# Three instead of eight transfers in flight at the start of the SyncE queue, in a fused retention and two-layer MoE kernel

## The chip, the cores and the metric

The kernel runs on one core of a Trainium2 chip. The metric is device time in microseconds (us); lower is better. Engines are named as in the profile: PE is TensorE, PEld its weight loads, DVE VectorE, ACT ScalarE, POOL GpSimd, SP SyncE. SP does no arithmetic here: it issues nearly all DMA transfers, in program order.

## The reference

```python
# attention with decay, B=4, H=8, S=768, D=64
for t in range(S):
    state = gamma * state + outer(k[:, :, t], v[:, :, t])
    y[:, :, t] = scale * (q[:, :, t] @ state)
x = y as 3072 tokens x 512
# first layer, d_ff 1024
h = x @ w_in
solu = h * softmax(h)
x = layernorm(solu) * g_ln @ w_out
# second layer, d_ff 2048
h = x @ w_in2
out = (h * cos(h)) @ w_out2
```

## The kernel before

The sequence is cut into chunks of 64 tokens. A step handles one chunk of two batches: scores of the chunk (`sc`, L394), the running state (`S`, L400), and the output from both (`y` or, for step 1, `hA`, L412), each as many 64x64 matmuls. There are 24 steps. Their results, split into a rounded and a remainder part (`xh`, `xl`), feed the first layer (L605, into `hA` and `hB`), whose weights `w1h` and `w1l` are made on the chip: raw words come into `big` (L478), ACT and DVE shift them together, ACT writes the rounded half (`w1h`) and DVE the remainder (`w1l`, L341). Later parts (L674, L851, L934, L936) are the rest of the two layers.

The order of all instructions is not written by hand. `Plan.add` records operations with their duration and their dependencies, and `Plan.order` (L117) plays them against a small model of the engines and of the DMA queue and emits them in that order. For DMA it holds that a transfer can start when the eighth before it has landed (`LANES`, L59, used at L169). The chip is held to the same rule by the semaphores: eight of them tell of landings, and each transfer waits for the earlier one that used its semaphore. Two of the first ones belong to constants that ACT issues (L366, L368).

Each step loads two transfers of 512 KB, the first with keys and queries ("kq"), the second with keys and values ("kv") (`load_step`, L357 to L368); there are four input buffers. A weight transfer (L478) is 511.8 KB. The start of the program is

```python
load_to(0)
load_to(2)
weights(2)
load_to(3)
weights(6)
```

so the first transfers of SP are, counted from 0: step 0 (0, 1), step 1 (2, 3), step 2 (4, 5), two weights (6, 7), step 3 (8, 9), six weights (10 to 15), steps 4 to 7 (16 to 22 and one more), with a small constant `gcol` (L504) close to the end.

Of the kernel before, what the change touches and what calls it, by code (L numbers as in the profile page):

```python
# [46 lines left out]
class Plan:  # L47
# [16 lines left out]
    STEP = 0.05  # L64
    LOOK = .1
    FIRST = (16, 0.96, 0.6)

    def __init__(self):
        self.ops = []
        self.alts = {}  # L70
        self.bulk = set()
        self.chain = False
        self.last = []
        self.keys = []
        self.writers = {}
        self.readers = {}
# [40 lines left out]
    def order(self):  # L117
        ops = self.ops
        n = len(ops)
        succ = [[] for _ in ops]  # L120
        need = [0] * n
        for i, o in enumerate(ops):
            need[i] = len(o[3])
            for d, full in o[3]:
                succ[d].append((i, full))
        last = None
        nxt = [None] * n
        for i, o in enumerate(ops):
            if o[0] == "PE":
                if last is not None:  # L130
                    nxt[last] = i
                last = i
        rank = [0.0] * n
        for i in range(n - 1, -1, -1):
            eng, occ, _, _, lat, _, xfer = ops[i]
            if i in self.alts and self.alts[i][1] < occ:
                lat -= occ - self.alts[i][1]
                occ = self.alts[i][1]
            tail = lat + self.SEM + (self.LEAD + xfer + self.LAND if xfer else 0)
            best = occ  # L140
            for s, full in succ[i]:
                best = max(best, rank[s] + (tail if full else 0))
            if nxt[i] is not None:
                best = max(best, rank[nxt[i]] + occ)
            rank[i] = best
        ready_at = [0.0] * n
        start = [None] * n
        free = {e: 0.7 for e in ("PE", "ACT", "DVE", "POOL", "SP", "HOOK")}
        pools = {e: [] for e in free}
        pe = [i for i, o in enumerate(ops) if o[0] == "PE"]  # L150
        port = [0.0, None]
        dma = 2.65
        begun = 0
        lanes = [0.0] * self.LANES

        def ready(i):
            if need[i] == 0 and ops[i][0] != "PE":
                pools[ops[i][0]].append(i)
                if i in self.alts:
                    pools[self.alts[i][0]].append(i)  # L160

        def begin(i, e):

            occ, prt = (ops[i][1], ops[i][5]) if e == ops[i][0] else (self.alts[i][1], self.alts[i][3])
            t = max(free[e], ready_at[i])
            if prt and port[1] != e:
                t = max(t, port[0])
            if ops[i][6]:
                t = max(t, lanes[-self.LANES])  # L169
                if i in self.bulk:  # L170
                    t = max(t, dma - self.BEHIND)
            return t, occ

        for i in range(n):
            ready(i)
        left = n
        out = []
        while left:
            best = None
            for e in free:  # L180
                if e == "PE":
                    c = []
                    for k, i in enumerate(pe[:self.WINDOW]):
                        if need[i] == 0:
                            t = max(free[e], ready_at[i])
                            c.append((max(free[e], ready_at[i] + self.MARGIN) + k * self.STEP, t, i))
                    if not c:
                        continue
                    _, t, i = min(c)
                    if best is None or t < best[0]:  # L190
                        best = (t, e, i)
                    continue
                else:
                    c = []
                    for i in pools[e]:
                        t, occ = begin(i, e)
                        if i in self.alts:
                            t2, occ2 = begin(i, self.alts[i][0] if e == ops[i][0] else ops[i][0])
                            if t2 + occ2 < t + occ - 1e-9:
                                continue  # L200
                        c.append((t, i))
                    if not c:
                        continue
                t0 = min(t for t, _ in c)
                pick = min((i for t, i in c if t <= t0 + self.LOOK), key=lambda i: -rank[i])
                t0 = next(t for t, i in c if i == pick)
                if best is None or t0 < best[0]:
                    best = (t0, e, pick)
            t, e, i = best
            eng, occ, _, _, lat, prt, xfer = ops[i]  # L210
            if e != eng:
                _, occ, _, prt = self.alts[i]
                lat = occ + 0.09
            if e == "PE":
                pe.remove(i)
            else:
                pools[eng].remove(i)
                if i in self.alts:
                    pools[self.alts[i][0]].remove(i)
            start[i] = t  # L220
            free[e] = t + occ
            if prt:
                port = [t + occ, e]
            done = t + lat + self.SEM
            if xfer:
                begun += 1
                boot = begun <= self.FIRST[0]
                if boot:
                    xfer *= self.FIRST[1]
                dma = max(dma, t + occ + self.LEAD) + xfer  # L230
                done = dma + self.LAND + (self.FIRST[2] if boot else self.LATE if i in self.bulk else 0.0)
                lanes.append(done)
            for s, full in succ[i]:
                need[s] -= 1
                ready_at[s] = max(ready_at[s], done if full else t)
                ready(s)
            out.append(self.alts[i][2] if e != eng else ops[i][2])
            left -= 1
        self.start = start
        self.end = max(s + o[4] for s, o in zip(start, ops))  # L240
        return out
# [3 lines left out]
def body(ctx: ExitStack, tc: tile.TileContext, qkv, consts,  # L245
# [3 lines left out]
    P = Plan()  # L249
# [80 lines left out]
        nc.gpsimd.memset(t, 0)  # L330
    make_identity(nc, ident)

    def dma(fn, size, r=(), w=(), occ=0.47, eng="SP", after=(), bulk=False):
        rows, row = size
        return P.add(eng, occ, fn, r, w, xfer=rows / 16 * max(0.046, row / 24.5e3), after=after, bulk=bulk)

    def act(out, in_, func, r, w, occ, lat=None, alt=None, **kw):
        return P.add("ACT", occ, lambda: nc.scalar.activation(out=out, in_=in_, func=func, **kw), r, w, lat, alt=alt)  # L338
# [18 lines left out]
    def load_step(n):  # L357

        bp, i = steps[n]
        for h, x in enumerate(("kq", "kv")):  # L360
            c = slice(2 * h, 2 * h + 2)
            dma(lambda h=h, c=c: nc.sync.dma_start(
                out=a_in[n % NA][:, c], in_=qkv[bp, i, :, h * 1024:h * 1024 + 1024].rearrange("p (c f) -> p c f", f=512)),
                (128, 4096), w=[("in", n % NA, x)])
            if n == 0 and h == 0:
                dma(lambda: nc.scalar.dma_start(out=c_all[:, 0:352], in_=consts[:, 0:352]), (128, 1408), w=[("cs",)], eng="ACT")  # L366
            if n == 1 and h == 0:
                dma(lambda: nc.scalar.dma_start(out=c_all[:, 352:608], in_=consts[:, 352:608]), (128, 1024), w=[("gat",)], eng="ACT")  # L368
# [881 lines left out]
```

## Time and profile before

| what | value |
|---|---|
| three runs | 825.86, 826.69, 828.76 us; median 826.69 |
| the profiled execution's own time | 827.25 us |
| its span, first to last instruction | 825.5 us |
| PE busy | 809.2 us, 98% of the span |
| DVE busy | 685.2 us, 83% |
| ACT busy | 504.6 us, 61% |
| HBM traffic | 226 GB/s over the span |

The span is the time between the first and the last instruction of the profiled execution; what lies around it makes up the rest of its own time. A busy share is an average over stages. A row of waits tells what ended the idle time of an engine; "issue" is time in which the engine waited for nothing that the profile shows.

### The profile page before, as it was taken

The numbers are of one execution on the slowest core, as the hardware profiler recorded it, in microseconds if no ns is written. First come the engines' busy times: TensorE is split into PE (matmuls) and PEld (weight loads), VectorE is DVE, ScalarE is ACT, GpSimd is POOL, SyncE is SP. The second block draws the span as 40 slices with busy tenths as digits, with TensorE's granted clock in tenths as the row PEclk, the third lists the DMA queues.
The fourth block names the chain that finished last, engine by engine and source line by source line (L and its number), as shares of the span: only waits on it lengthen the run. The fifth ranks groups of instructions, "written<-read, shape, count | busy, mean of one in ns | idle before, by whom it ended". The sixth has DMA issues, their size and how long they took to land.

```text
span 825.5 us, 17746 instructions
## 1 busy us (share of the span) xinstructions
PE 809.2 (98%) x6652; PEld 682.4 (83%) x6652; DVE 685.2 (83%) x1269; ACT 504.6 (61%) x908; POOL 48.5 (6%) x55
## 2 busy tenths in 40 slices
PE   4999999999999999999999999999999999999998
PEld 4788888888888888788888888888888888888887
DVE  4799978889888677449999996899999949989975
ACT  3789856656666466346686563666846546665453
POOL 2131201101101000000000000000000000000000
PEclk9999999999999999999999999999999999999999
DMA  9894799999976638247666779766657696666664
GB/s 346 333 333 143 259 306 295 320 288 293 330 264 226 222 161 308 90 133 197 193 205 189 215 209 283 241 193 195 203 187 227 195 283 199 192 194 190 187 190 98
DMA packets 93509, 188.12 MB, mean 228 GB/s; under 512 B 9712, under 2 KB 25328, under 8 KB 93424
## 3 DMA queue, kind: packets, MB, share of 16 engines
q1 hardware_dynamic: 92816, 186.41, 70.8%
q8 instruction: 53, 0.87, 0.4%
q10 hardware_dynamic: 608, 0.57, 0.2%
q14 instruction: 32, 0.26, 0.1%
HBM read 145.01 MB, written 41.94 MB: 226 GB/s over the span
## 4 chain that ended last, share of the span: by engine, by line
PE 95%; DMA 2%; DVE 1%; issue 1%; SPq 0%; ACT 0%; DVEq 0%
PE U L851 28%; PE hA L605 14%; PE y L674 12%; PE pa L934 10%; PE U L934 8%; PE pa L936 5%; PE y L412 4%; PE U L936 4%; PE tr L650 2%; PE hB L605 2%; PE tr L674 2%; PE sc L394 1%; DMA wr<-wd 1%; PE S L400 1%; DMA raw<-y1d 1%
## 5 line engine op out<-in xcount | busy, mean ns | idle before, releaser
L879 ACT ACTIVATE gh<-A 128x512 fp32r<-128x512 f32 x168 | 106.2, 632 | 94.6 <-PE pa L934 48.2
L881 DVE TENSOR_TENSOR gl<-A,gh 128x512 fp32r<-128x512 f32 x168 | 114.6, 686 | 13.5 <-ACT gh L879 11.3
L674 PE MATMUL y<-lt,o1h 128*128 128x512 f32 x304 | 102.1, 399 | 0.0
L934 PE MATMUL pa<-wr,gh 128*128 128x512 f32 x372 | 101.6, 394 | 0.0
L888 DVE TENSOR_TENSOR A<-A,A 128x512 f32<-128x512 f32 x120 | 81.0, 684 | 0.7
L934 PE MATMUL U<-wr,gh 128*128 128x512 f32 x288 | 78.6, 394 | 0.0
L934 PEld LDWEIGHTS pa<-wr,gh 128*128 128x128 f32 x372 | 63.9, 189 | 8.9
L674 PEld LDWEIGHTS y<-lt,o1h 128*128 128x128 f32 x304 | 57.1, 188 | 12.6 <-ACT ys L679 0.3
L605 PE MATMUL hA<-w1h,xh 128*128 128x512 f32 x160 | 64.5, 403 | 0.2 <-DVE u L349 0.2
L936 PEld LDWEIGHTS pa<-wr,gl 128*128 128x128 f32 x372 | 57.2, 189 | 8.0
L605 PE MATMUL hA<-w1h,xl 128*128 128x512 f32 x160 | 62.6, 391 | 0.0
L605 PE MATMUL hA<-w1l,xh 128*128 128x512 f32 x160 | 62.5, 391 | 0.0
L936 PE MATMUL pa<-wr,gl 128*128 128x256 f32 x372 | 59.4, 281 | 0.0
L674 PE MATMUL y<-lt,o1l 128*128 128x512 f32 x152 | 59.3, 390 | 0.0
L338 ACT ACTIVATE st<-wt 128x512 fp32r<-128x512 f32 (+1 forms) x60 | 35.7, 600 | 36.3 <-DMA wd<-st 24.6
L341 DVE TENSOR_TENSOR st<-wt,st 128x512 fp32r<-128x512 f32 (+1 forms) x60 | 41.2, 689 | 18.4 <-ACT st L338 18.1
L934 PEld LDWEIGHTS U<-wr,gh 128*128 128x128 f32 x288 | 49.3, 189 | 6.6
L936 PEld LDWEIGHTS U<-wr,gl 128*128 128x128 f32 x288 | 44.2, 188 | 6.1
L412 PE MATMUL y<-s,in 64*64 64x64 f32 x736 | 45.0, 226 | 1.6 <-DVE s L341 1.6
L936 PE MATMUL U<-wr,gl 128*128 128x256 f32 x288 | 45.7, 280 | 0.0
L412 PEld LDWEIGHTS y<-s,in 64*64 64x64 f32 x736 | 36.4, 138 | 9.7 <-issue 6.0
L412 PE MATMUL y<-x,st 64*64 64x64 f32 x672 | 40.6, 218 | 2.7 <-issue 2.7
(177 smaller groups left out, 1943.4 us busy)
## 6 DMA issues: line engine op xcount, KB each, us to landing
wr<-wd SPq DMA_DIRECT2D x168, 256.0 KB, 2.9
wr<-td SPq DMA_DIRECT2D x168, 256.0 KB, 2.9
in<-qkv_dram SPq DMA_DIRECT2D x48, 512.0 KB, 6.3
wd<-st SPq DMA_DIRECT2D x28, 512.0 KB, 5.6
td<-st SPq DMA_DIRECT2D x24, 512.0 KB, 3.6
raw<-w_in_dram SPq DMA_DIRECT2D x16, 511.8 KB, 6.1
raw<-w_out_dram SPq DMA_DIRECT2D x16, 511.8 KB, 5.0
y1d<-ys SPq DMA_DIRECT2D x24, 256.0 KB, 3.8
```

Source lines behind the costliest of these rows:

```text
L338: return P.add("ACT", occ, lambda: nc.scalar.activation(out=out, in_=in_, func=func, **kw), r, w, lat, alt=alt)
L341: return P.add("DVE", occ, lambda: nc.vector.tensor_tensor(out=out, in0=a, in1=b, op=op), r, w, port=port)
L412: nc.tensor.matmul(out=ybank(n)[0][o, j], lhsT=a[r, j], rhs=b[r, j], start=not part, stop=bool(part) or not later)
L605: nc.tensor.matmul(out=h, lhsT=a[:, k], rhs=w1[lo][k][c], start=(k + m == 0), stop=(k == KD - 1 and m == 2))
L650: nc.tensor.transpose(out=trs[s][:, t * 128:(t + 1) * 128], in_=us[(4 * g + t) % UBUF].rearrange("p c f -> p (c f)")[:, j * 128:(j + 1) * ...
L674: nc.tensor.matmul(out=y1(), lhsT=w[:, j, ds], rhs=lts[j][:, a], start=(j + m == 0), stop=(j == K1 - 1 and m == 2))
L851: nc.tensor.matmul(out=U(), lhsT=p2["wr"][w][:, kk, lo], rhs=p2["x"][m][xl][:, kk], start=(kk + q == 0 and m in (0, 1, 4)), stop=(kk == 1 ...
L879: P.add("ACT", 0.54, lambda: nc.scalar.activation(out=p2["gh"][i], in_=src(), func=AF.Copy), [key], [("gh", i)], after=(*p2["cos_hook"], * ...
L881: P.add("DVE", 0.6, lambda: nc.vector.tensor_tensor(out=p2["gl"][i], in0=src(), in1=p2["gh"][i].bitcast(F32), op=ALU.subtract), [key, ("gh ...
L888: P.add("DVE", 0.6, lambda: nc.vector.tensor_tensor(out=f(o), in0=f(a), in1=f(b), op=alu), [("A", q, s) for q in (a, b)], [("A", o, s)], p ...
L934: nc.tensor.matmul(out=o, lhsT=p2[x][g][:, c], rhs=p2["wr"][w].rearrange("p a b c -> p (a b c)"), start=fresh, stop=False, skip_group_chec ...
L936: nc.tensor.matmul(out=o[:, 0:256], lhsT=p2[x][g][:, c], rhs=v[:, 0, :], start=False, stop=s == 7, skip_group_check=True)
```

## The change

The planner gets a third number set, `FLIGHT = (24, 3, 1.3)`. For the first 24 transfers that SP issues, `Plan.order` lets a transfer start only when the third before it has landed by its model, less 1.3 us, and the helper `dma` adds a real dependency: the transfer waits for the landing of the third one before it on SP. From the 25th on the old rule stands alone. Transfers that ACT issues are neither counted nor held.

```diff
+    FLIGHT = (24, 3, 1.3)
...
+        flown = []
...
             if ops[i][6]:
                 t = max(t, lanes[-self.LANES])
+                if e == "SP" and self.FLIGHT[1] <= len(flown) < self.FLIGHT[0]:
+                    t = max(t, flown[-self.FLIGHT[1]] - self.FLIGHT[2])
...
                 lanes.append(done)
+                if e == "SP":
+                    flown.append(done)
...
+    flight = []
+
     def dma(fn, size, r=(), w=(), occ=0.47, eng="SP", after=(), bulk=False):
         rows, row = size
-        return P.add(eng, occ, fn, r, w, xfer=rows / 16 * max(0.046, row / 24.5e3), after=after, bulk=bulk)
+
+        def start():
+            ins = fn().ins
+            n = len(flight)
+            if Plan.FLIGHT[1] <= n < Plan.FLIGHT[0]:
+                tc.add_manual_dep(ins, flight[n - Plan.FLIGHT[1]],
+                                  mybir.DependencyInfo(mybir.DependencyClass.Sync, mybir.DependencyReason.DATA), reason="in flight")
+            flight.append(ins.name)
+        return P.add(eng, occ, start if eng == "SP" else fn, r, w, xfer=rows / 16 * max(0.046, row / 24.5e3), after=after, bulk=bulk)
```

Lines after the helper stand 16 lower in the changed file: L362 becomes L378, L478 becomes L494, L504 becomes L520. On PE, DVE, ACT and POOL every instruction stands where it stood.

The first place is the start of the SP queue. `in_162` to `in_165` are the four input buffers, `big_116` on are the weights; "waits" names the semaphores, and DMAHW0 to 7 are those of landings. Before:

```order
L362 DMA in_162<-qkv_dram 128x1024 x2
L362 DMA in_163<-qkv_dram 128x1024 x2
L362 DMA in_164<-qkv_dram 128x1024 x2
L478 DMA big_116<-w_in_dram 128x2047 [waits DMAHW0_49]
L478 DMA big_117<-w_in_dram 128x2047 [waits DMAHW1_49]
L362 DMA in_165<-qkv_dram 128x1024 [waits DMAHW2_49]
```

And in the change:

```order
L378 DMA in_162<-qkv_dram 128x1024 x2
L378 DMA in_163<-qkv_dram 128x1024
L378 DMA in_163<-qkv_dram 128x1024 [waits DMAHW0_49]
L378 DMA in_164<-qkv_dram 128x1024 [waits DMAHW2_49]
L378 DMA in_164<-qkv_dram 128x1024 [waits DMAHW4_49]
L494 DMA big_116<-w_in_dram 128x2047 [waits DMAHW5_49]
L494 DMA big_117<-w_in_dram 128x2047 [waits DMAHW6_49,DMAHW1_49]
```

Nothing moved here; waits came in. Transfer 3 now waits for transfer 0, transfer 4 for transfer 1 and so on, where before the first six were issued without a wait.

The second place is the end of the 24, also on SP. Before:

```order
L362 DMA in_164<-qkv_dram 128x1024 [waits DVE_49,DMAHW7_49,PE_49,Activation_49]
L362 DMA in_165<-qkv_dram 128x1024 [waits DMAHW0_49,PE_49,Pool_49]
L504 DMA gcol_75<-consts_dram 128x8 [waits DMAHW1_49]
L362 DMA in_165<-qkv_dram 128x1024 [waits DMAHW2_49,PE_49,Activation_49]
L362 DMA in_162<-qkv_dram 128x1024 [waits DMAHW3_49,PE_49,Pool_49]
```

And in the change:

```order
L378 DMA in_164<-qkv_dram 128x1024 [waits DVE_49,DMAHW4_49,PE_49,Activation_49]
L378 DMA in_165<-qkv_dram 128x1024 [waits DMAHW5_49,PE_49,Pool_49]
L378 DMA in_165<-qkv_dram 128x1024 [waits DMAHW6_49,PE_49,Activation_49]
L520 DMA gcol_75<-consts_dram 128x8
L378 DMA in_162<-qkv_dram 128x1024 [waits PE_49,Pool_49]
```

The small `gcol` moved behind the last transfer of step 7, and is now the first transfer without the new wait. This is the only instruction of the program that moved.

## Rows read from the trace of the kernel before

**Rows 1.** Busy time by stretch, whole program; columns as in the first line.

```profile
core 0: us, PE busy (x) PEld busy (x) DVE busy (x) ACT busy (x) POOL busy (x), PEclk, DMA share, GB/s
5.50:21.88 16.38, 10.10 (x351) 9.31 (x351) 8.59 (x15) 5.43 (x12) 3.83 (x3) 1.00 1.02 405
25.93:817.50 791.57, 790.83 (x6229) 665.60 (x6228) 671.60 (x1242) 493.52 (x885) 43.05 (x43) 1.00 0.71 224
```

**Rows 2.** Timeline of PE: start, length, instruction, idle before it and what ended it.

```profile
15.54 0.21 PE L394 MATMUL sc<-in 64*64 64x64 f32 x1 [1.14 <-issue]
...
21.88 0.27 PE L412 MATMUL y<-x,st 64*64 64x64 f32 x1 [2.72 <-issue]
...
23.30 0.79 PE L605 MATMUL hB<-w1h,xh 128*128 128x512 f32 x1
```

**Rows 3.** Busy time in PE's first idle stretch and in two later ones; columns as above.

```profile
14.40:15.54 1.14, 0.00 (x2) 0.00 (x0) 0.69 (x3) 0.00 (x0) 0.00 (x0) 1.00 1.01 410
...
15.54:19.16 3.62, 2.81 (x128) 2.54 (x127) 2.83 (x3) 1.90 (x3) 1.28 (x1) 1.00 1.03 423
...
21.88:32.54 10.66, 10.66 (x127) 8.71 (x128) 9.55 (x14) 9.25 (x17) 1.81 (x1) 0.84 1.03 418
```

**Rows 4.** DMA queues (packets, MB, share of 16 engines), 15.54 to 19.68 us.

```profile
q1 hardware_dynamic: 480, 1.74, 103.0%
```

**Rows 5.** DMA queues, 19.68 to 20.63 us.

```profile
q8 instruction: 1, 0.02, 6.2%
```

**Rows 6.** DMA queues, 32.54 to 32.98 us, then 32.98 to 34.08 us.

```profile
q1 hardware_dynamic: 84, 0.15, 90.1%
...
q8 instruction: 1, 0.02, 6.1%
```

**Rows 7.** DMA queues, 10.2 to 13.1 us, then 13.1 to 14.1 us.

```profile
q1 hardware_dynamic: 329, 1.18, 101.0%
...
q8 instruction: 1, 0.02, 5.8%
```

**Rows 8.** PE's low-clock stretch; columns as in rows 1.

```profile
22.52:25.93 3.41, 3.41 (x24) 2.81 (x21) 3.06 (x6) 3.35 (x8) 0.00 (x0) 0.50 1.04 422
```

**Rows 9.** Timeline of SP's issues: start, length, transfers.

```profile
0.74 3.48 SPq L362 DMA_DIRECT2D in<-qkv_dram  x6
5.50 0.82 SPq L478 DMA_DIRECT2D big<-w_in_dram  x2
...
8.96 7.45 SPq L478 DMA_DIRECT2D big<-w_in_dram  x6
17.39 7.80 SPq L362 DMA_DIRECT2D in<-qkv_dram  x7
26.05 0.33 SPq L504 DMA_DIRECT2D gcol<-consts_dram  x1
35.33 0.80 SPq L362 DMA_DIRECT2D in<-qkv_dram  x2
```

**Rows 10.** Issue to landing (last number, us) of the transfer issued at 16.1, then 80.2.

```profile
big<-w_in_dram SPq DMA_DIRECT2D x1, 511.8 KB, 10.0
...
in<-qkv_dram SPq DMA_DIRECT2D x1, 512.0 KB, 3.9
```

**Rows 11.** Issue to landing of the transfers issued at 43.45 and 44.41.

```profile
in<-qkv_dram SPq DMA_DIRECT2D x1, 512.0 KB, 5.7
...
big<-w_out_dram SPq DMA_DIRECT2D x1, 511.8 KB, 7.0
```

**Rows 12.** Timelines of ACT, DVE and PE: use of the last first-layer weight.

```profile
31.01 0.79 ACT L338 ACTIVATE top<-big 128x512 f16<-128x512 bf16 x1
...
32.74 1.88 DVE L341 TENSOR_TENSOR w1l<-big,w1h 128x512 fp32r<-128x512 f32 x3
...
37.94 0.39 PE L605 MATMUL hB<-w1l,xh 128*128 128x512 f32 x1
```

## The prediction

> **What bounds the kernel now.** I read the busy time by stretch first, then PE's timeline where PE is idle, then the DMA queues around those idle stretches, last the issues of SP with their landings. From 25.93 to 817.5 us PE is busy for 790.83 of 791.57 us [rows 1]: behind the start the kernel is PE from end to end, with nothing to gain from DMA. From 5.50 us, when the first transfer has landed and frees SP's seventh issue [rows 9], to 21.88 us PE is busy for 10.10 us of 16.38 [rows 1]. The change touches the first 24 transfers of SP, which are issued up to about 35 us [rows 9], so its whole effect must come out of the start, and what PE gains there is carried to the end, since PE hardly waits later.
>
> Two idle stretches of PE in the start are put down to no engine and no data: 1.14 us before 15.54 and 2.72 us before 21.88, both "issue" [rows 2]. Between them stand 128 matmuls and 127 weight loads, 255 instructions [rows 3]; the next 255 end at 32.54 us [rows 3]. A stop after about 256 instructions says that PE ran out of fetched program. The DMA queues show the fetch: from 15.54 to 19.68 us there is only data on the queues [rows 4], and then one packet of the instruction queue, which takes 6.2% of 16 engines for 0.95 us, so about 0.94 us on one engine [rows 5]. PE goes on at 21.88, 1.25 us after the packet's end. I read it so: as a block of 256 instructions begins, the next one is asked for; at 15.54 it was asked for and lay 4.14 us behind data. In the block that begins at 32.54, when SP's queue drains, no instruction packet is there for 0.44 us and then it is [rows 6]: unloaded the wait is at most 0.5 us. Before the first stop, a packet begins at 13.1 us [rows 7]; its block, counted back 256 instructions from 14.40, began at about 10.2 us, so it waited some 2.9 us.
>
> A third loss follows from the second stop: from 22.52 to 25.93 us the granted clock is 0.50, the lower level of 1.2 GHz [rows 8]. PE had been idle for 2.72 us just before. After the stop of 1.14 us the clock stayed at 1.00 [rows 3]. The low stretch costs half its length, 1.7 us.
>
> **The change part by part.**
>
> *Waits on SP.* With eight in flight the queue issues one transfer per landing: six weights from 8.96 to 16.1 us and then seven inputs in 7.80 us, of which the last takes 0.33, so (7.80 - 0.33) / 6 = 1.245 us per transfer [rows 9], at 10.0 us from issue to landing [rows 10]. Alone, a transfer lands in 3.9 us [rows 10]. Three in flight at 3.9 us each would give one per 1.3 us. That is the main point: three are just enough to keep the rate, and the other five only stood in line. Transfers 0 to 2 are issued as before; transfer 3, issued when 0 lands (5.5 us, when the old queue issued its seventh transfer [rows 9]), still finds 1 and 2 ahead of it, so its landing hardly moves. I take 1.3 us, 0.05 more than now, and bound it below by 1.245 and above by 2.2 (a rival, below). By the last weight, transfer 15, that is 13 x 0.05 = 0.7 us.
>
> Who waits for it: transfer 15 was issued at 16.1 and landed at 26.1 [rows 9, 10]; ACT reads it at 31.01 [rows 12], 4.9 us later; DVE finishes the last remainder at 34.62 and PE needs it at 37.94 [rows 12], 3.3 us later. So 0.7 us is hidden, even when PE comes almost 4 us sooner. Behind the waiting SP stand only transfers; the next one that PE sets free is issued at 35.33 [rows 9], later than the 24 are out. Cost: zero. If this cover were gone, each microsecond of lateness would be one of PE. The moved `gcol` is issued some 10 us later, at about 36 us, by a queue that has no other use for the moment: zero.
>
> *The fetch.* With eight in flight the wait of 4.14 us less the 0.44 unloaded is 3.7 us, at 1.245 us per transfer three transfers' worth of packets, not the seven or eight that were queued. With three in flight, the queue holds two transfers when a third is released, and has worked off most of one more before that third one's packets come; so between one and a little over two transfers. I take 1.65 x 1.245 + 0.44 = 2.5 us. Bounds: 0.5 (an empty queue) and 4.14 (nothing changes). The second stop shrinks by 4.14 - 2.5 = 1.65 us to 1.07, the first by 2.9 - 2.5 = 0.4 to 0.74. With the first landing I expect no change and bound it by 0.5 us sooner, from 4.8 us (issued at 0.74, with the seventh issue at 5.50 [rows 9]) against 3.9 alone.
>
> Here a rule of the notes speaks against the change. The Trainium skill, page "DMA: Bandwidth & Descriptors", section "Queues, rings and completion order", says that each DMA engine goes round its queues packet by packet, where such a packet is a bundle of typically 9 to 17 descriptors. By that rule the fetch waits for one bundle however many transfers stand behind it, and the change would leave the stops as they are. The trace has 3.7 us of data ahead of the fetch; whether a bundle or the whole queue is ahead it doesn't tell.
>
> *The clock.* A stop of 1.07 us is shorter than the one of 1.14 us after which the clock stayed high. I count the 1.7 us as saved.
>
> **Sum.** -1.65 - 0.4 - 1.7 = -3.75 us. Against the profiled execution's 827.25 us (a span of 825.5 and 1.75 around it) this gives **823.5 us**. Its time lies 0.56 above the median of 826.69; I leave the sum where it is, because some of the runs may lack the low clock, and the saving with it.
>
> **The rivals.**
>
> *Partly.* The stops shrink, but the clock falls all the same (or the wait shrinks by only half a microsecond): -2.05 us alone, or about -1 to -2.4: 824.2 to 826. For it speaks that only two stops, of 1.14 and 2.72 us, show what the clock tolerates.
>
> *Unchanged.* The wait for the fetch depends on what the DMA engine has in hand, not on the queue: 826.7, as before. For it speaks that 3.7 us is less than half of the 10.0 us that a data transfer then waits [rows 10]; against it that the wait went down to 0.44 us while the queue drained. The Trainium skill, page "Runtime: NRT & Kernel Launch", section "Instruction fetch mechanics", has blocks of 256 instructions, as the trace does, and calls the cost of crossing from one to the next mostly hidden; the 2.72 us here [rows 2] are not.
>
> *Slower: the rate falls.* Two transfers issued at 43.45 and 44.41 landed after 5.7 and 7.0 us [rows 11], at 49.15 and 51.4: 2.2 us apart, with three in flight or fewer. At that pace transfer 15 lands 13 transfers behind transfer 2. Transfer 2 lands at 8.96 (it frees the issue at 8.96 [rows 9]), so 8.96 + 13 x 2.2 = 37.6 instead of 26.1. The last remainder is ready 34.62 - 31.01 = 3.6 us later, at 41.2; PE, 3.75 us ahead, wants it at 34.2 and waits 7 us: 823.5 + 7 = 830.5. The point from which this decides: at 34.2 - 3.6 = 30.6 us for transfer 15 it starts to cost, a pace of 1.66 us per transfer; at 1.95 the gain is eaten. Against it: those transfers were issued in a burst into an idle queue, and 3.9 us alone [rows 10] says 1.3.
>
> That the new waits don't act is no rival: the order shows them on SP's instructions.
>
> **How the numbers follow.** About 0.3% (2.5 us) is what a measurement of this kernel can tell from no change, so faster means below 824.2 and slower above 829.2. Chances: the forecast (821 to 824.2) 0.52, partly 0.23, unchanged 0.15, slower 0.10. Faster 0.52; within 0.3% 0.23 + 0.15 = 0.38; slower 0.10. The range: if both stops vanish (3.86), the clock holds (1.7) and the first landing comes 0.5 sooner, the time is 821.2; I put the lower end at 821.0. The upper end of 827.6 takes in the unchanged case around the profiled 827.25. The slower rival and a little at the lower end are left out.
>
> **What would show it.** Right: SP's issue to landing for transfers 6 to 22 falls from 10 us to about 4 at a pace near 1.3 us; PE's second "issue" stop is about 1 us, and the instruction packet comes 2 to 3 us after the block's beginning; no stretch with the clock at 0.50 after 20 us; PE starts on the first layer (first L605) near 21 us in place of 23.30 [rows 2]. Wrong: the stops keep their 1.14 and 2.72 us; or the queue's pace goes beyond 1.66 us and PE waits for `w1l` between 30 and 40 us. If time is gained at the start and the total doesn't follow, a later engine took it, and PE's 0.74 us of idle time after 25.93 would have grown.

## The result, and the profile after

The change is slower: a median of 832.39 us (830.34 to 833.00, six runs) against 827.82 us for the kernel before beside it (825.86 to 829.11, six runs). The ratio is 1.0053, with a 95% interval of 1.0035 to 1.0071. The profiled execution took 832.86 us with a span of 831.1 us, 5.6 us more than the span before. The forecast was 823.5 us with an upper end of 827.6, and slower had a chance of 0.10. Line numbers are now those of the changed file, mostly 16 higher than before.

Three views say where the 5.6 us came from. First what PE waited for in the whole trace of the change (total, times, longest):

```profile
PE sc L410 <- DMA in<-qkv_dram: 6.0, 2, 5.4
PE hB L621 <- DVE u L365: 2.9, 1, 2.9
PE y L428 <- issue: 2.2, 1, 2.2
PE sc L410 <- issue: 1.8, 1, 1.8
```

The two "issue" stops, for which the prediction was made, are 1.8 and 2.2 us and sum to 3.97 in the timeline; before they were 1.14 and 2.72 [rows 2], 3.86 in sum. Nothing was gained there. Two waits are new. The first row holds the wait for the first landing (5.4 us, 5.5 before) and one of 0.67 us for an input; the second is a wait of 2.92 us for DVE. They stand in the timeline of PE:

```profile
16.05 0.21 PE L410 MATMUL sc<-in 64*64 64x64 f32 x1 [1.80 <-issue]
...
21.84 0.27 PE L428 MATMUL y<-x,st 64*64 64x64 f32 x1 [2.17 <-issue]
...
23.09 0.79 PE L621 MATMUL hB<-w1h,xh 128*128 128x512 f32 x1
...
35.16 0.27 PE L410 MATMUL sc<-in 64*64 64x64 f32 x2 [0.67 <-DMA in<-qkv_dram]
...
46.92 0.80 PE L621 MATMUL hB<-w1h,o1h 128*128 128x512 f32 x1 [2.92 <-DVE u L365]
```

PE starts the first layer at 23.09 us, 0.21 us sooner than before [rows 2]. By 50 us it is more than 5 us behind. The windows of the change (columns as in rows 1) answer to [rows 1, 3, 8]:

```profile
5.37:21.84 16.47, 10.10 (x351) 9.31 (x351) 7.67 (x15) 5.45 (x12) 3.99 (x3) 1.00 0.86 299
...
22.67:26.09 3.42, 3.42 (x19) 2.72 (x16) 3.18 (x5) 2.96 (x8) 0.00 (x0) 0.50 0.83 299
26.09:46.57 20.48, 17.24 (x310) 13.85 (x309) 12.31 (x17) 12.09 (x26) 4.15 (x3) 1.00 0.86 277
46.57:49.98 3.41, 3.06 (x7) 2.48 (x8) 3.41 (x7) 2.16 (x6) 0.00 (x0) 0.50 0.75 199
49.98:823.10 773.12, 772.01 (x5912) 650.39 (x5912) 653.83 (x1219) 479.77 (x857) 39.98 (x40) 1.00 0.71 225
```

The low stretch of the clock after the second stop is still there, as long as before (3.42 us against 3.41 [rows 8]). A second one, 3.41 us at 0.50, goes with the new wait of 2.92 us; for its first 0.35 us PE was still idle, and half of the 3.06 us in which PE was busy is 1.5 us. Before 46.57 us the queue moved 277 to 299 GB/s at a share of 0.83 to 0.86, where it had moved over 400 at a full share [rows 1, 3]. From 49.98 us on PE is idle for 1.1 us of 773. Where the 5.6 us arose shows when each matmul is compared with the same one before: PE is 0.05 us ahead at 34 us, 0.93 behind past the first new wait (0.67 us of idle time and 0.31 us more until PE had its pace again), 3.92 past the second, 5.35 past the second low stretch, and 5.58 at the end.

The wait of 2.92 us is named after DVE, but DVE itself waited. Its timeline in the change:

```profile
39.29 1.23 DVE L639 TENSOR_REDUCE sm<-hB 128x1 f32<-128x1024 f32 x1
45.44 0.29 DVE L399 TENSOR_SCALAR in<-in,c_all 128x128 f32<-128x128 f32 x1 [4.93 <-DMA in<-qkv_dram]
45.65 1.22 DVE L365 SCALAR_TENSOR_TENSOR u<-u,hB 128x1024 f32<-128x1024 f32 x1
```

L399 scales keys of step 6, whose second transfer (number 21) landed at 45.4 us; before it had landed at 33.8. In DVE's order this scaling stands ahead of the product u (L365), which frees `hB` for PE. So one late input held up a product that doesn't use it.

The transfers themselves, SP's timeline of the change (start, length, transfers):

```profile
0.74 8.05 SPq L378 DMA_DIRECT2D in<-qkv_dram  x6
...
18.16 9.70 SPq L494 DMA_DIRECT2D big<-w_in_dram  x6
29.17 15.40 SPq L378 DMA_DIRECT2D in<-qkv_dram  x8
```

The six weights 10 to 15 go out at (9.70 - 0.33) / 5 = 1.87 us per transfer, where the inputs before went out at 1.245 [rows 9]. The DMA view of 12 to 32 us of the change says the same from the landing side (queue: packets, MB, share; then transfers, KB each, median us from issue to landing):

```profile
q1 hardware_dynamic: 1543, 5.61, 81.9%
...
big<-w_in_dram SPq DMA_DIRECT2D x7, 511.8 KB, 5.5
in<-qkv_dram SPq DMA_DIRECT2D x4, 512.0 KB, 5.6
```

5.5 us with three in flight is one per 1.83 us. The prediction had taken 3.9 us for each of the three.

### The profile page after: what moved, and what is told of

Read it like the earlier page. It is cut to its first block, busy times and chain, and to the rows that moved or that the text cites. A ratio compares the mean times of both kernels' runs of the same rounds, so it can differ in the third digit from the quotient of the medians.

```text
span 831.1 us, 17746 instructions
## 1 busy us (share of the span) xinstructions
PE 810.9 (98%) x6652; PEld 683.6 (82%) x6652; DVE 682.4 (82%) x1269; ACT 504.9 (61%) x908; POOL 49.8 (6%) x55
## 4 chain that ended last, share of the span: by engine, by line
PE 91%; DMA 7%; DVE 1%; issue 0%; SPq 0%; ACT 0%; DVEq 0%; ACTq 0%
PE U L867 28%; PE hA L621 13%; PE y L690 11%; PE pa L950 10%; PE U L950 8%; PE pa L952 5%; PE U L952 4%; DMA in<-qkv_dram 4%; PE y L428 4%; PE tr L666 2%; PE tr L690 2%; DMA big<-w_in_dram 2%; PE hB L621 2%; DMA raw<-y1d 1%; PE sc L410 1%; DMA wr<-wd 1%
## 5 line engine op out<-in xcount | busy, mean ns | idle before, releaser
L897 DVE TENSOR_TENSOR gl<-A,gh 128x512 fp32r<-128x512 f32 x168 | 115.1, 689 | 13.7 <-ACT gh L895 11.6
L357 DVE TENSOR_TENSOR st<-wt,st 128x512 fp32r<-128x512 f32 (+1 forms) x60 | 39.0, 653 | 20.5 <-ACT st L354 20.3
```

Source lines behind the costliest of these rows:

```text
L357: return P.add("DVE", occ, lambda: nc.vector.tensor_tensor(out=out, in0=a, in1=b, op=op), r, w, port=port)
L897: P.add("DVE", 0.6, lambda: nc.vector.tensor_tensor(out=p2["gl"][i], in0=src(), in1=p2["gh"][i].bitcast(F32), op=ALU.subtract), [key, ("gh ...
```

## The experiments

Where only a condition and a k are given, the kernel keeps the change's order of instructions and alters nothing but which transfers wait: the helper's condition becomes `if a <= n < b`, and the landing waited for is that of transfer n - k. The times of the kernel before are those measured beside each. A ratio is the one on record, with its 95% interval; it is not the quotient of the two medians.

**Four and six in flight.**

```diff
-    FLIGHT = (24, 3, 1.3)
+    FLIGHT = (24, 4, 1.3)
```

and (24, 6, 1.3) in the second.

> Four in flight instead of three for the first 24 SP transfers; every engine's order is that of the change. Rate theory (with three in flight the DMA engines run dry, 1.9 us per transfer in place of 1.245, and PE's new waits come from late inputs): 4 in flight at 5 to 6 us from issue to landing give 1.25 to 1.5 us per transfer; transfer 22 lands at 34 to 38 us in place of 46.7; PE's waits of 0.67 and 2.92 us and the second low-clock stretch vanish; time 826.5 to 829. Rival (any added wait on SP costs, or what was lost is the fetch of PE's program): 831 to 833.

> Six in flight instead of three. Rate theory: 1.245 us per transfer as with eight, transfer 22 lands near 35 us, time as before the change, 826.5 to 828.5. Rival (the added waits themselves cost): still above 830.

Four: 826.15 us against 826.89, ratio 0.9996 (0.9981 to 1.0010). Six: 827.21, ratio 0.9997 (0.9983 to 1.0010). Neither can be told from before. The DMA view of 12 to 32 us, before:

```profile
q1 hardware_dynamic: 2274, 8.28, 101.7%
...
in<-qkv_dram SPq DMA_DIRECT2D x7, 512.0 KB, 10.1
```

four in flight:

```profile
q1 hardware_dynamic: 1858, 6.77, 96.4%
...
in<-qkv_dram SPq DMA_DIRECT2D x7, 512.0 KB, 6.4
```

and six in flight:

```profile
q1 hardware_dynamic: 2271, 8.27, 101.7%
...
in<-qkv_dram SPq DMA_DIRECT2D x7, 512.0 KB, 7.8
```

Six keep the full rate, four lose a fifth of it, three a third. With four, transfer 22 landed at 39.6 us, later than the 34 to 38 of the forecast, and transfer 21 landed 4.5 us later than before. PE paid nothing for it: its second stop is again 2.72 us and no wait for an input came in. That brackets the reserve: 4.5 us of lateness at transfer 21 are free, 11.6 are not.

**One in flight.** `if 1 <= n < 24`, k = 1.

> One in flight for the first 24, order of the change, to measure the fetch of PE's program: only one transfer is ever ahead of it. If the fetch waits behind queued data: its packet begins at most 1.8 us after the block of 256 instructions begins (0.5 unloaded and 1.25 for one transfer), against 4.1 with eight and 3.4 with three. If the wait has another cause: 2.5 us or more as in the change. The time is not the point; one transfer per 3.9 us puts transfer 15 near 60 us, so 850 us or more.

One run: 873.24 us. SP's timeline gives the pace of single transfers, and the DMA view of 36.6 to 40.6 us shows one of them (busy share of the engines in 40 slices of 0.1 us; it was issued at 36.63 us):

```profile
40.18 18.25 SPq L494 DMA_DIRECT2D big<-w_in_dram  x6
```

```profile
DMA  0000000002888587979889816233012000000000
```

(18.25 - 0.33) / 5 = 3.58 us each. Nothing moves for 0.9 us; then most engines work for 1.4 us; then for 0.8 us only a few still do; the landing follows 0.5 us later. The fetch of instructions, asked for at the beginning of a block as in [rows 4, 5], waited 0.6 and 0.8 us here.

**The key scalings behind u.** Order of the change, but the eight scalings of steps 6 and 7 (ACT and DVE) are emitted after the product u of row block 2.

```diff
+        pairs = list(zip(ids, out))
+        kept = [x for x in pairs if x[0] not in self.hold]
+        at = 1 + next(k for k, x in enumerate(kept) if x[0] == self.mark)
+        out = [f for _, f in kept[:at] + [x for x in pairs if x[0] in self.hold] + kept[at:]]
...
+                if n in (6, 7):
+                    P.hold.append(o)
```

> Three in flight as in the change, but the eight scalings of the keys of steps 6 and 7 (which read the inputs that land last) are moved on ACT and DVE behind the third row block's product u. In-order theory (an instruction that waits for a late input holds up DVE and ACT, and with them PE): pace stays at 1.9 us per transfer, PE's wait of 2.92 us near 47 us and the low-clock stretch behind it vanish; time 827 to 829. Rival (PE needs the late data themselves): the wait turns up at another place, time 831 to 833.

831.42 us, ratio 1.0056 (1.0035 to 1.0078): as slow as the change, so taking the scalings out of the way does not bring the time back. What PE waited for in this kernel:

```profile
PE sc L420 <- DMA in<-qkv_dram: 7.0, 2, 5.4
PE hA L631 <- DVE u L373: 2.5, 4, 1.3
...
PE hB L631 <- DVE u L373: 0.6, 1, 0.6
```

The wait for u that was aimed at fell from 2.9 to 0.6 us. But PE, not held there, stood 1.6 us for the input of step 4 itself, and 2.5 us in sum behind other products u (0.2 before). At 60 us PE is only 1.23 us behind the kernel before, not 5.35 as in the change, and at the end 4.13; most of what came in between are waits for u of 1.29 us at 74.7 and of 0.82 at 153.8. The stops for instructions were shorter in this execution too (1.71 and 1.35 us) and no low stretch of the clock followed, so not all of the better start is owed to the move. Whether the later waits come from the late inputs or from the new order on DVE and ACT was not tried.

**Three in flight for half of the 24.** k = 3 for transfers 3 to 11, and for 12 to 23.

> Order of the change; three in flight holds only for transfers 3 to 11, from 12 on the queue fills to eight again. Lateness theory: PE pays nothing for late transfers until they are later than what the engines have in reserve. In the change transfer 11 landed at 25.7 us, about 4.7 us later than before, and behind it the queue should run at 1.25 us per transfer, so the last input of step 6 (transfer 21) lands near 39 us, not at 45.4; with four in flight throughout, a lateness of 4.5 us there cost PE nothing. So no DVE or ACT wait of over 1 us for inputs of steps 4 to 7 that reaches PE, no PE wait of 0.67 or 2.92 us, no second low-clock stretch, and 825.5 to 828.0 us. Rival, each held transfer costs its share: nine of 21 held transfers, about 0.4 of the loss of 4.6 us, 828.7 us.

> Order of the change; three in flight holds only for transfers 12 to 23. Lateness theory: the pace there is 1.9 us, plus some 2 us while the queue runs down from eight to three, so transfer 21 lands near 41.5 us, 7.7 us later than before and about 1 us inside the reserve: no PE wait of 2.92 us, 825.5 to 828.0 us. The first PE stop stays near 1.1 us, the second one is 1.3 to 2.7. Rival, each held transfer costs its share: twelve of 21, 829.3 us, with PE waiting for inputs between 34 and 48 us.

First half: 828.68 us against 827.25, ratio 1.0018 (1.0007 to 1.0029). Second half: 829.36, ratio 1.0027 (1.0013 to 1.0041). Both forecasts of the lateness theory (up to 828.0) were missed, and the times lie where a cost in proportion to the held transfers puts them. That is an agreement of numbers alone: four in flight holds 20 transfers at no cost, and below seven transfers held to two in flight cost more than all 21 of the change. In the second half's trace PE is 0.78 us behind at 60 us, and the rest of its 3.10 us at the end came from waits for DVE and ACT between 125 and 335 us. The large waits are gone from both traces, as foretold; several smaller ones, most of 0.3 to 0.6 us, have come. What PE waited for with the second half held (a selection):

```profile
PE y L428 <- issue: 3.0, 1, 3.0
PE tr L666 <- DVE lt L677: 1.1, 1, 1.1
...
PE hA L621 <- DVE u L365: 0.6, 2, 0.4
PE S L416 <- issue: 0.5, 1, 0.5
```

So there is no single threshold, as I had assumed. The last row is a third stop for instructions, at 47.0 us: transfers that were put off fill the queue when a later block's fetch is asked for (it waited 3.3 us there, where before it had waited 1.5).

**A short queue only while the two fetches wait.** k = 3 for transfers 8 to 17; k = 2 for 9 to 15.

> Order of the change; three in flight holds only for transfers 8 to 17, those that stand in the queue while PE stops for its program at 15 and 21 us. If the short queue does shorten the wait for the fetch: the two waits from a block's beginning to its instruction packet fall from 4.1 and 4.0 to 2.5 to 3.4 us, the two stops in sum from 3.9 to 2.0 to 3.2 us, and since transfer 21 lands no later than 40 us nothing is lost: 823.5 to 826.0 us, with 1.7 us more where no low-clock stretch follows. Rival, the wait for the fetch doesn't depend on how many transfers stand in line, only on the phase in which it comes: stops of 3.5 to 4.5 us in sum and 826 to 828 us.

> Order of the change; only two in flight, for transfers 9 to 15. If the wait for the fetch follows the number in flight, it falls to 1.3 to 2.2 us (one transfer in flight gave 0.8, three gave 2.5 to 3.4), both stops go to under 0.5 us, the clock stays up, and at a pace near 2.3 us transfer 15 lands about 7 us late, at 33, which the change itself (33.0) bore without a PE wait for a weight: 822 to 824.5 us. Rival, no such dependence: stops of 3 us or more in sum, and 826 to 829 us with the late weights.

830.26 us (ratio 1.0026, 1.0011 to 1.0040) and 834.18 us (1.0079, 1.0061 to 1.0097). Both forecasts of the time were missed, while the fetch came out close to what was foretold: with three in flight it waited 2.39 and 3.31 us and the stops were 1.38 and 1.08 us; with two it waited 1.24 and 1.58 us and the stops were 1.11 and 0.26 us, the first of them longer than the 0.5 of the forecast. In both the clock stayed up at 20 to 26 us. The DMA queues in the kernel with two in flight, 14.97 to 16.21 us (from the block's beginning, data only) and then 16.21 to 17.50 us:

```profile
q1 hardware_dynamic: 72, 0.23, 45.6%
...
q8 instruction: 1, 0.02, 6.2%
```

With two in flight PE was 4.6 us ahead of before by 21.4 us. Then it gave all of it back, most of it in one wait, and more (PE's timeline; two in flight, transfers 9 to 15):

```profile
38.08 0.37 PE L410 MATMUL sc<-in 64*64 64x64 f32 x2 [7.02 <-DMA in<-qkv_dram]
```

With three for transfers 8 to 17 the same row reads 3.55 us, and a low stretch of the clock goes with it in both. The input is that of step 4: it is issued behind the last weights and was the next thing to be late.

**Shorter still.** k = 2 for transfers 9 to 11 alone; k = 3 for 9 to 11 alone.

> Order of the change; two in flight for transfers 9 to 11 alone, eight again from 12 on (issued from 19.7 us). If a short queue shortens the fetch and only lateness takes the gain back, as the run with two in flight for transfers 9 to 15 says (waits of 1.2 and 1.6 us, stops of 1.11 and 0.26, clock up, PE 2.85 us ahead at 24 us, then 7.0 us lost on a late input): the same waits and stops, the clock up at 22 to 26 us, the first input of step 4 (transfer 16) landing at 30 to 31 us, before PE wants it at 31.5, and 823.8 to 825.5 us, 2 to 3 us below before. Rival, lateness still costs: transfer 16 lands after 31.5 us, PE waits for it, and 826 to 828.5 us.

> Order of the change; three in flight for transfers 9 to 11 alone, eight again from 12 on (issued from about 17.2 us, before the second fetch is asked for). If the fetch waits for what stands in the queue when it is asked for: first wait 2.3 to 3.2 us, second one 3.5 to 4.2 as before, the second stop over 1.5 us and a low-clock stretch after it, 826 to 828 us. Rival, any pause in the queue serves both fetches: second wait under 3 us, and 824 to 826 us.

Two: 828.42 us against 827.03, ratio 1.0014 (1.0002 to 1.0027), where 823.8 to 825.5 had been forecast. Three: 826.92, ratio 1.0001 (0.9987 to 1.0014). Both do at the start what the prediction wanted of the change. The profiled execution of the first is its fastest, 825.30 us, and no measure of its median. For the second (profiled at 827.23 us) PE's stops are 1.22 and 0.80 us, the clock is 1.00 from 21 to 26 us, no late input stops PE, and the n-th matmul of its trace stands 3.5 us ahead of the same matmul before at 34 us and 2.6 us ahead at 60 us. From 365 us on it is level. What PE waited for there:

```profile
PE tr L666 <- DVE lt L677: 1.4, 2, 1.0
PE hA L621 <- DVE u L365: 1.4, 3, 0.8
...
PE S L416 <- issue: 0.5, 1, 0.5
```

In the same view of the kernel before, the first two waits are 0.5 and 0.2 us in sum. They lie at 127 to 150 us and at 331 us, and they ate most of the lead. In my forecast for this kernel I had also tied the second stop to the second fetch. It hangs on the first one, asked for at 15.5 us (1.79 us with three in flight); the second fetch waited 5.24 us, and the block of 9 us ahead of it hid that.

**Less work for PE at the start.** Twelve products of the first layer left out, in the kernel before and in the change.

```diff
             for m in ms:
                 a, lo = ((xh, 0), (xl, 0), (xh, 1))[m]
+                if n == 1 and k in (1, 2):
+                    continue
```

> The kernel before, with 12 first-layer products of row block 1 left out (its second and third quarter of the depth, so its output lacks them): 12 x 0.227 = 2.7 us less work for PE, all of it before 41 us, the order else unchanged. The prediction's premise, that what PE gains at the start is carried to the end: 2.7 us below before, about 824.3 us. Rival, from the run with three in flight for transfers 9 to 11, which was 2.6 us ahead at 60 us and level with before from 365 us on: PE gives most of it back in waits for DVE between 120 and 160 us and near 330 us, and the time is 825.8 to 827.3.

> The change, with the same 12 products left out (2.7 us less for PE before 42 us). If late inputs set the time of the change, PE only waits longer for them (the waits before the scores of step 4, near 35 us, and before the products behind u, near 47 us, grow by 2 us or more in sum) and the time stays within 0.8 us of the change's: 831.6 to 832.8 us. Rival, PE's own work still sets it and the late inputs cost their waits alone: 2.7 us less, about 829.7 us.

Before without the products: 825.27 us against 827.06, ratio 0.9975 (0.9961 to 0.9989), 1.8 us less for 2.7 us of work: between the two forecasts. In its trace PE is 2.5 us ahead at 60 us and 1.2 at the end. The change without them: 832.25 us, where the change had 832.39; against the kernel before beside each, the ratios are 1.0057 (1.0038 to 1.0077) and 1.0053. In the time nothing came through. The timeline of PE in it:

```profile
27.34 0.50 PE L623 MATMUL hB<-w1h,xh 128*128 128x512 f32 x1 [1.36 <-ACT w1h L354]
...
35.27 0.37 PE L410 MATMUL sc<-in 64*64 64x64 f32 x2 [3.77 <-DMA in<-qkv_dram]
...
46.53 0.50 PE L623 MATMUL hB<-w1h,o1h 128*128 128x512 f32 x1 [1.32 <-DVE u L365]
...
143.23 0.50 PE L623 MATMUL hA<-w1h,xh 128*128 128x512 f32 x1 [0.96 <-DVE u L365]
```

The second and third wait were 0.67 and 2.92 us in the change; their sum grew by 1.5 us and not by the 2 of the forecast. The first is new: PE, which at 23.4 us was 3.3 us ahead of before, waited for a late weight, for which ACT had itself waited 2.43 us. So late transfers took part of the 2.7 us. But not all: from 50 to 100 us PE is 1.8 us ahead of the same matmul of the change, and level with it from 200 us on. The last wait shown is the largest of those that took the rest. The time fell into the forecast range, then, but only partly for the reason given.

## Why the prediction was wrong

**The pace of three in flight: this step failed.** "Three in flight at 3.9 us each would give one per 1.3 us. That is the main point." They gave one per 1.83 to 1.87 us, because in company each took 5.5 us. From the DMA view of each kernel's held stretch (time for the 0.524 MB of a transfer, which is 512 times 1024 bytes, by the MB moved; and median issue to landing):

| in flight | us per 512 KB | issue to landing, us |
|---|---|---|
| 8 (before) | 1.27 | 10.1 |
| 6 | 1.27 | 7.8 |
| 4 | 1.55 | 6.0 to 6.4 |
| 3 (the change) | 1.87 | 5.5 |
| 2 (transfers 9 to 15, 16 to 28 us) | 2.38 | 4.6 |
| 1 (SP's pace) | 3.58 | 3.5 |

The row of two in flight rests on this view:

```profile
q1 hardware_dynamic: 725, 2.64, 67.3%
...
big<-w_in_dram SPq DMA_DIRECT2D x5, 511.8 KB, 4.6
```

Dividing the time alone by the number in flight gives 1.19 us for three, and by that three would be enough. The two bounds, 1.245 and 2.2, did hold the pace; I took the one nearest to a single transfer, though the row of two transfers issued close to each other [rows 11] was the nearer case and said 5.7 and 7.0 us. The rate was lost in two places. The engines' share fell from 101.7 to 81.9%, and the time per packet grew: 81.9% of 320 engine-microseconds over 1543 packets is 170 ns, and 101.7% over the 2274 packets before is 143 ns. The tail of the single transfer suggests a cause for the first: a landing waits for the last of the engines, and with a short queue the others have nothing else. Why packets take longer was not tried.

**Who waits for it: this step failed too.** I looked at `w1l` alone and put the cost at zero. PE never waited for a late `w1l` in the change: DVE had the last one ready at 38.0 us, 3.4 us later than before, and PE came to it at 38.9. The late inputs of steps 4 and 6, the last things in the held queue, cost 0.67 us directly and 2.92 us through DVE, and the second low stretch 1.5 us. The slower rival had the right mechanism, a falling rate, and its point of decision (1.66 us) was passed. It too had PE wait for a weight, for a PE that is ahead; in the change PE wasn't. Where it was, in the change without the twelve products, a weight wait of 1.36 us did come.

**The fetch: right in kind, too small to matter.** I took 2.5 us for the wait with three in flight. The 0.44 us that I took off as the unloaded wait was none: at 32.54 us two inputs were still in flight, and the engines were 90.1% busy [rows 6]. The trace before also held a nearer case than those I used: the block begun at 46.25 us, with three in flight, got its packet after 3.10 us. Of the blocks begun between 10 and 22 us, 17 in eight kernels began with three in flight: their fetches waited 0.5 to 5.7 us, 2.7 in the mean. With eight in flight six of them waited 2.9 to 4.2 us, 3.6 in the mean; with four to seven, twelve waited 2.6 to 5.2, 3.5 in the mean; with two, three waited 1.2 to 1.6; with one, two waited 0.6 and 0.8. So the wait does fall with the queue, plainly so at two and one, and the rival "unchanged" is wrong in kind. The count from a block's first matmul is rough: in three kernels the packet at 28 to 32 us began 0.7 to 1.6 us ahead of it. By the arbitration rule of the Trainium skill, page "DMA: Bandwidth & Descriptors", section "Queues, rings and completion order", it would not have fallen; by these runs it does. The fall from eight to three is 0.9 us in the mean, not 1.65, under a scatter that is larger. In the change's profiled execution the two waits that matter were 3.74 and 3.37 us. The first stop grew by 0.66 us and the second shrank by 0.55.

**The clock: a term that hung on the stop.** With the second stop at 2.17 us the clock fell as before; where experiments brought that stop to 1.35 us or less (seven kernels), it stayed up, and where it was 1.48 us, with a data wait of 0.39 us close behind, or more, it fell. The condition I gave held as far as these runs go, and it was not met. The term itself was a little large: in the traces without the low stretch PE gained 1.5 us on the kernel before between 22 and 26 us, not 1.7.

**"What PE gains there is carried to the end, since PE hardly waits later": not so in most of these runs.** PE's 790.83 busy of 791.57 us [rows 1] says that nothing was lost later at the old start, not that a sooner start would find DVE ready. A lead of 2.6 us at 60 us vanished with three in flight for transfers 9 to 11, and of 2.5 us with the products left out 1.2 remained in the trace (by the medians 1.8 of the 2.7 us, and by the interval 0.9 to 3.2, so this run alone does not refute the premise). But losses grew as well. Of the thirteen other traces, one execution each, twelve lost a further 0.2 to 2.9 us against before between 60 us and the end, whether PE was ahead at 60 us (six in flight: 1.79 us ahead, then 0.31) or behind (second half held: 0.78 behind, then 3.10; the change: 5.35, then 5.58). In one the lead grew (two for 9 to 11: 1.10, then 1.96). The waits there are for DVE and ACT; why they differ so from kernel to kernel was not tried. So even with the forecast's gains at the start, the change would hardly have been 3.75 us faster. Of the whole kernels level with before at 60 us or ahead of it, four in flight, six in flight and three for 9 to 11 equal it in time, two for 9 to 11 is a little slower, and none of the versions beats it.

## What to carry to other kernels

The time of a transfer alone, divided by the number in flight, is a bound for the pace and not a forecast: measure the latency in company, or leave twice what that division asks for. If you slow a queue, list every consumer behind the last held transfer, in the order in which each engine takes its work, because an engine that waits for a late tile also holds up what stands behind it. A bound engine without idle time shows only that nothing was lost behind the start as it is: after a sooner start or a later one, look at what it waits for behind the start, and don't carry the difference to the end unseen.

## What the runs showed of the hardware

With 512 KB transfers, one is done in 3.5 us, of which 0.9 pass before the first packet; six in flight gave the rate that eight give, and four did not. The Trainium skill, page "DMA: Bandwidth & Descriptors", section "Anatomy of one DMA — SWDGE (gpsimd) path", gives a fixed cost of about 2 us for a transfer issued from GpSimd; the 3.5 us here less the 1.27 us that 512 KB take in a full queue leave 2.2, close to it, for transfers issued from SP. The trace splits the 3.5 us otherwise: 0.9 before the first packet, 2.2 for the packets with their tail, 0.5 up to the landing.

In four kernels, six in flight among them, PE didn't stop at 15 us; it had run slower instead. Windows of 13.30 to 14.00 us, first before, then six in flight (columns as in rows 1):

```profile
13.30:14.00 0.70, 0.70 (x61) 0.70 (x57) 0.02 (x1) 0.37 (x2) 0.00 (x0) 1.00 0.97 398
```

```profile
13.30:14.00 0.70, 0.70 (x40) 0.70 (x36) 0.08 (x1) 0.69 (x2) 0.02 (x1) 1.00 0.99 398
```

40 matmuls in the window in place of 61, at a granted clock that is recorded as 1.00 in both. Matmuls there came at nearly twice the distance (0.20 to 0.21 us per eight, 0.117 before), with six in flight until about 20.5 us, in two of the four only until about 16 us. The stops that follow were shorter by about as much: six in flight shows 0.59 us for the second stop with a fetch wait of 3.91 us. So a short "issue" stop alone is no proof of a short fetch wait; the spacing of the matmuls ahead of it has to be looked at. What slowed them is open.
